# Attention with a gated expert mixture on one core: stores on another queue, transposes and sums in another order

## The chip, the cores and the metric

The kernel runs on one core of one Trainium2 chip. The metric is the time of one execution on the device, in microseconds (us). The engines are named as the profile names them: PE (TensorE; PEld is its loading of weights), DVE (VectorE), ACT (ScalarE), POOL (GpSimd) and SP (SyncE, which here only issues transfers). Each engine works through its own stream of instructions in the order in which they were written; between engines, semaphores hold an instruction until its data are there. A DMA that is issued by an engine is an instruction in that engine's stream, and what it moves goes through the queue of that engine.

## What is computed

The input `x` has 2048 tokens of 1024 features. The output is a gated mixture of two branches:

```
x  = A_x                                   # [2048, 1024]
g  = sigmoid(sum(x * gate_w))              # one number for each token
a  = softmax(q k^T / sqrt(32)) v @ wo      # 32 heads of 32, q, k, v = x @ wqkv
b  = expert lookup: 32 heads; in each, x @ w_q gives two scores over 8 keys each;
     the best pair picks a row of u and of v: sum over heads of gelu(x . u[e]) * v[e]
out = g * a + (1 - g) * b
```

All of it is float32. TensorE multiplies numbers of a shorter form (`F32R`), so each operand is split into a high part (a rounded copy) and a low part (operand minus high part), and a product is three products of parts.

## The kernel before

The program is written out by hand in one order (`tc.manual_schedule()`); what an engine does first is what comes first in the text. It has five stages.

**q and k** (trace: 6 to 378 us). The projections of q and k are computed in units: unit `u` takes one chunk of 128 output features for q and for k and half of the tokens, as a 2 x 2 block product by Strassen's scheme (Winograd's form): seven products P1 to P7 of 12 matmuls each, in the order P1, P5, P6, P2, P7, P3, P4, instead of eight. Units 0 and 8 (`KC` is 8, the units of a half) are computed plainly, as there the operands for the tokens are made; units 1 to 7 and 9 to 15 run in `unit(u)` (L473). Around the products:

- The weights of the next unit, `v = u + 1`, are prepared during unit `u`. `turns` says after which product which part is made: a name with `+` is a sum of raw blocks on VectorE (`w_sum`, L216), a name without is a split into high part (ScalarE, `w_hi`) and low part (VectorE, `w_lo`). `ready(name)` (L482) does the turn of a product. In most units a turn has a sum or a split; in units 1 and 9 the turns begin only at P2 and are denser.
- VectorE adds the products into the four output blocks `c1`, `u7`, `u4`, `u2`, from PSUM. After P2, P7, P3 and P4 one block is done, and `evac` (L248) takes it out: the high part on ScalarE, then `run_late()`, then the low part on VectorE. Put on the list `late` are the squares of the block (ScalarE, for a bound on the scores; they also end the use of the PSUM bank) and the two stores of high and low part to the DRAM tensors of q or k, 256 KB each, on ScalarE's queue. They are issued at the next `run_late()`, in the next evacuation or after P1 of the next unit. High and low parts have three buffers each (`ev`, `bufs=3`); a product takes the next of six PSUM banks.
- `fold` (L320) is another computation, put between the products to fill TensorE: the router's weights `wq` (1 MB for each of 32 steps, loaded on SP's queue into four buffers of 512 KB) times differences of keys. Two steps a call, all four quarters of a PSUM bank filled after four steps; then ScalarE copies the bank (L336), and `fold_t` (L341), called between P5 and the rest of a later unit, transposes the copy with four small matmuls on TensorE (L348), has ScalarE copy the result into the buffer named `u7` (L351), and stores it to DRAM (`WPD`) through GpSimd's queue. The block `u7` of the unit goes into the same buffer after P7 (L530). Units with an entry in `MID_FOLDS` (4, 11, 13) have a second fold, after P2.
- `hooks` puts other work at named places of certain units, for example the splitting of the second half of the tokens in unit 7.

**Router** (378 to 471 us). For 16 tiles `t` of 128 tokens, `router_mm(t)` (L702, 24 matmuls) gives the scores, and `router_step(t)` the choice of the best keys, in four steps on VectorE and GpSimd that lag behind each other. Between the tiles stand: the splitting of the tokens' third and fourth quarter (`split_rx`, at t = 1, 2, 3, 5; loads `load_rx` on SP's queue); the norms of q and k from the squares (`norms`, VectorE and a square root on ScalarE, t = 2; `spread_norms`, t = 3); `bound` (L769, t = 4), which adds up the norms with small matmuls (L771, L773), writes the bound to `cbits` and a shift for each head to DRAM; loads of the v weights on SP's queue (t = 4). At t = 8 `exact_maxima` reads `cbits` and branches.

**Values** (471 to about 631 us), **attention** (about 631 to 1657 us: for each head, scores into a ring of PSUM banks, exponentials on ScalarE, products with v, row sums), and the **output projection** (from there to the end). At the last head's end the row sums are computed on TensorE (L1335), copied by ScalarE (L1372) and stored with a DMA on SP's queue (`norm_sums`, L1369). `load_r` reads them back in another layout, `norm_r` takes reciprocals (L1383) and stores them (`RD`), and `load_rb` reads these broadcast over the partitions; the last 128 features of the attention's output are scaled with them before they can be multiplied by `wo` (L1506).

Of the kernel before, what the change touches and what calls it, by code (L numbers as in the profile page):

```python
# [18 lines left out]
H = 32  # L19
KC = D // 128  # L20
HC = KC // 2
NT = S // 128
NQ = S // 512
# [8 lines left out]
def gated_mha_peer_kernel(ctx, tc, xT, wqkv, wv, wo, wq, k12, ug, v, out):  # L32
# [8 lines left out]
    nc = tc.nc  # L41
# [14 lines left out]
    SMD = [dram.tile([4, S], F32, name=f"smd{g}") for g in range(G)]  # L56
# [17 lines left out]
    def dma(dst, src, queue=nc.sync):  # L74
        a, b = (ap.bitcast(F32) if ap.dtype == F32R else ap for ap in (dst, src))
        return queue.dma_start(a, b)  # L76
# [60 lines left out]
    def lo_of(parts, src):  # L137
        nc.vector.tensor_tensor(out=parts[1], in0=src, in1=parts[0].bitcast(F32), op=OP.subtract)  # L138
# [86 lines left out]
    def w_hi(u, name, src=None):  # L225
        hi_of(w_place(name), wraw[u][src or name])

    def w_lo(u, name, src=None):
        lo_of(AW[name], wraw[u][src or name])

    def w_parts(u, *names):
        for name in names:
            w_hi(u, name)
            w_lo(u, name)


    late = []
# [7 lines left out]
    def squares(out, src, which, c, n):  # L245
        nc.scalar.activation(out, src, AF.Square, accum_out=sq[:, which, c, n:n + 1])  # L246

    def evac(which, c, n, src, ps):  # L248
        hi, lo = (ev.tile([128, 512], F32R, name=part) for part in ("hi", "lo"))
        hi_of((hi, lo), src)  # L250
        run_late()
        lo_of((hi, lo), src)
        late.append((squares, ps, src, which, c, n))
        for dst, t in zip(QKD[which], (hi, lo)):
            late.append((dma, dst[128 * c:128 * c + 128, n * 512:(n + 1) * 512], t, nc.scalar))

    def load_kq(h, tiles):
        K, Q = tiles
# [27 lines left out]
    def product(name):  # L286
        ps = bank_at(prod_no[0] % 6)
        prod_no[0] += 1
        a, b = (m[f] for m, f in zip((AW, X), FACTORS[name]))
        for k in range(HC):  # L290
            for i, j in ((0, 0), (0, 1), (1, 0)):
                nc.tensor.matmul(ps, a[i][:, k, :], b[j][:, k, :],  # L292
                                 start=(k == 0 and i == j == 0), stop=(k == HC - 1 and i == 1))
        return ps
# [46 lines left out]
    def fold_t():  # L341
        if not pending:
            return
        gi, wt = pending.pop(0)
        b, dh = divmod(gi, 2)
        pt = bank_at(7)
        for dc in range(4):
            nc.tensor.transpose(pt[:, dc * 128:(dc + 1) * 128], wt[:, dc * 128:(dc + 1) * 128], ident)  # L348
        wt2 = ev.tile([128, 512], F32, name="u7", bufs=1)[:, :448].rearrange(
            "p (a q r) -> p a q r", a=4, q=4)  # L350
        nc.scalar.activation(wt2, pt.rearrange("p (a q r) -> p a q r", a=4, q=4)[:, :, :, :28], AF.Copy)  # L351
        dma(WPD[:, 4 * dh:4 * dh + 4, 112 * b:112 * b + 112], wt2.rearrange("p a q r -> p a (q r)"),
            nc.gpsimd)
# [119 lines left out]
    def unit(u):  # L473
        p, c, v = u // KC, CHUNK[u], u + 1
        n0 = TOK0[p] // 512
        seven = v < NUNIT and v != KC
        turns = (dict(P2=("S1+", "S3+", "A11"), P7=("S1", "S2+", "S2"), P3=("S4+", "A12"), P4=("S3", "S4"))
                 if u % KC == 1 else
                 dict(P1=("S1+", "S3+", "A11"), P5=("S1", "S2+"), P6=("S2", "S4+"), P2=("A12",),
                      P7=("S3",), P3=("S4",), P4=("A22",)))  # L480

        def ready(name):  # L482
            if not seven:
                return
            for part in turns.get(name, ()):
                if part[-1] == "+":
                    w_sum(v, part[:-1])
                else:
                    w_parts(v, part)

        def hook(name):
            for f, *a in hooks.pop((u, name), []):
                f(*a)

        def place(name):
            return ev.tile([128, 512], F32, name=name, bufs=1)

        def add(out, a, b):
            nc.vector.tensor_tensor(out=out, in0=a, in1=b, op=OP.add)  # L499

        p1 = product("P1")
        c1 = place("c1")
        nc.scalar.activation(c1, p1, AF.Copy)
        run_late()
        hook("P1")
        ready("P1")
        p5 = product("P5")
        fold_t()
        hook("P5")
        ready("P5")  # L510
        p6 = product("P6")
        u2, u4 = place("u2"), place("u4")
        hook("P6")
        add(u2, c1, p6)
        add(u4, u2, p5)
        ready("P6")
        if v + 1 < NUNIT and v + 1 != KC:
            load_w(v + 1)
        p2 = product("P2")
        hook("P2-")  # L520
        add(c1, c1, p2)
        evac(0, c, n0, c1, p2)
        if u in MID_FOLDS:
            fold()
        hook("P2")
        ready("P2")
        p7 = product("P7")
        hook("P7-")
        u7 = place("u7")
        add(u7, u4, p7)  # L530
        add(u2, u2, p7)
        evac(1, c, n0 + 1, u7, p7)
        hook("P7")
        ready("P7")
        p3 = product("P3")
        hook("P3-")
        add(u4, u4, p3)
        evac(0, c, n0 + 1, u4, p3)
        hook("P3")
        ready("P3")  # L540
        p4 = product("P4")
        add(u2, u2, p4)
        evac(1, c, n0, u2, p4)
        if u in FOLDS:
            fold(u != KC - 2)
        hook("P4")
        ready("P4")
# [143 lines left out]
    sm = Pool("sm")  # L691
# [67 lines left out]
    def norms():  # L759
        nc.vector.tensor_reduce(blk, ident.rearrange("p (j r) -> p j r", j=4), axis=AX.X, op=OP.max)  # L760
        nc.vector.tensor_reduce(amax, sq, axis=AX.X, op=OP.max)
        nc.vector.tensor_mul(pr, amax[:, 0, :], amax[:, 1, :])
        nc.scalar.activation(pr, pr, AF.Sqrt)

    def spread_norms():
        nc.vector.tensor_mul(prm, pr[:, :, None].to_broadcast([128, KC, 4]),
                             blk[:, None, :].to_broadcast([128, KC, 4]))

    def bound():  # L769
        pb = bank()  # L770
        nc.tensor.matmul(pb[:H, 0:1], prf, ones[:, 0:1], start=True, stop=True)  # L771
        pb2 = bank()
        nc.tensor.matmul(pb2[:1, :H], ones[:, 0:1], prf, start=True, stop=True)  # L773
        nc.vector.tensor_reduce(cbits, pb2[:1, :H], axis=AX.X, op=OP.max)
        cneg = bw.tile([H, 1], F32, name="cneg")
        nc.scalar.activation(cneg, pb[:H, 0:1], AF.Copy, scale=-1.0)
        for r in range(2):
            sh = bw.tile([H, 512], F32R, name=f"sh{r}", bufs=1)
            if r == 0:
                nc.vector.tensor_copy(sh, cneg.to_broadcast([H, 512]))  # L780
            else:
                nc.vector.memset(sh.bitcast(F32), 0.0)
            dma(SHD[:, r, :].rearrange("h (n s) -> h n s", n=4), sh[:, None, :].to_broadcast([H, 4, 512]))
# [63 lines left out]
    def load_rx(n, i):  # L847
        rx[n, i] = load_quarter(n, i, rz.tile([128, HC, 512], F32, name="rx", bufs=2))
# [7 lines left out]
    for t in range(NT - 1):  # L856
        router_mm(t)
        if t == 8:

            exact_maxima()  # L860
        router_step(t)
        if t == 2:
            norms()
        if t == 3:
            spread_norms()
        if t == 4:
            bound()
            load_wv(0, "xh0")
            load_wv(1, "xl0")
        if t in (1, 2, 3, 5):  # L870
            ni, ki = {1: (2, 0), 2: (2, 1), 3: (3, 0), 5: (3, 1)}[t]
            split_rx(ni, ki)
            if ni == 2:
                load_rx(3, ki)
        if t == 6:
            rz.close()
        if t >= 8 and t % 2 == 0:
            ni, ki = divmod(t // 2 - 4, 2)
            in_parts(f"B{ki + 1}{2 - ni}", x_place(f"x{'hl'[ki]}{1 + ni}"), WR[ki, 1 - ni])
# [486 lines left out]
        dma(OD[g][32 * j:32 * j + 32, :].rearrange("d (q s) -> q d s", q=NQ), o)  # L1366


    def norm_sums(h, ps):  # L1369
        g, j = divmod(h, 4)  # L1370
        o = wk.tile([128, 512], F32, name="ssb")
        ins = nc.scalar.activation(o, ps, AF.Copy)  # L1372
        dma(SMD[g][j:j + 1, :].rearrange("o (q s) -> (o q) s", q=NQ), o[::32, :])
        return ins


# [50 lines left out]
    todo = {}  # L1427
# [4 lines left out]
    for h in range(H):  # L1432
        base = h * NT
        g, j = divmod(h, 4)
# [14 lines left out]
    for k in range(2 * KC):  # L1449
        c = slice(k % 2 * D // 2, (k % 2 + 1) * D // 2)  # L1450
# [134 lines left out]
    sm = pso.tile([128, 512], F32, name="o")  # L1585
# [3 lines left out]
    for kc in range(1, KC - 1):  # L1589
        split_hi(kc + 1)  # L1590
        if kc == 1:
            norm_sums(H - 1, sm)
            load_r(G - 1)
            for n in range(2):
                load_at(n)
            pso.close()
        split_lo(kc)
        wo_mm(pa, 0, [kc], False, False)
# [155 lines left out]
```

## Time and profile before

| | |
|---|---|
| median of 3 runs | 1849.5 us (1849.14 to 1852.69) |
| profiled execution, its own time | 1848.97 us |
| its span, first to last instruction | 1847.2 us |
| mean granted TensorE clock | 0.996 |
| DMA | 345.24 MB, mean 187 GB/s |

The profiled execution is the slowest core's, here the only one's. The span is shorter than the time by 1.77 us, which lie around it. Busy times of the engines are unions of their instructions; an engine's idle time before an instruction is put down to what released it. The granted clock is the share of TensorE's clock pulses that the throttle let through in a stretch, 1.00 being full speed. Lines such as L348 are lines of the kernel above. In the chain of waits and in the timelines, times are from the start of the span.

### The profile page before, as it was taken

What the parts mean: (1) busy time and instruction counts of PE and PEld (TensorE: products, weight loads), DVE (VectorE), ACT (ScalarE), POOL (GpSimd) and SP (SyncE); (2) the same over time, 40 slices, a digit from 0 to 9 for tenths busy, and PEclk for the clock granted to TensorE, in tenths of its full rate; (3) what the DMA queues carried; (4) which work ended last, traced back from release to release, by engine and by line L of the source; (5) the groups of instructions that cost most, each with busy time, mean ns of one, the idle gap of its engine ahead of it and who ended that gap; (6) DMA issues with size and microseconds to landing.
All of it is one profiled execution on the core that took longest, in us unless ns stands there. A gap on an engine that the chain in (4) does not pass through costs nothing.

```text
span 1847.2 us, 26455 instructions
## 1 busy us (share of the span) xinstructions
PE 1823.2 (99%) x10083; PEld 1103.8 (60%) x10083; DVE 1460.9 (79%) x1258; ACT 1313.8 (71%) x1716; POOL 162.1 (9%) x230
## 2 busy tenths in 40 slices
PE   9999999999999999999999999999999999999999
PEld 6677777778888744444444444444444444447787
DVE  7765875679976888888888888888888888885575
ACT  5544554522243599999999999999999999992221
POOL 1000000024201200000000000000000000010000
PEclk9999999999999999999999999999999999999999
DMA  7787788843248777777777777778777777776872
GB/s 261 228 286 249 235 256 293 249 137 105 80 154 268 238 168 165 164 159 178 163 184 161 178 179 166 178 167 186 164 182 163 169 161 178 185 135 171 279 174 79
DMA packets 135633, 345.24 MB, mean 187 GB/s; under 512 B 17168, under 2 KB 57904, under 8 KB 116112
## 3 DMA queue, kind: packets, MB, share of 16 engines
q1 hardware_dynamic: 95696, 193.41, 35.4%
q0 software_dynamic: 17984, 112.36, 28.1%
q10 hardware_dynamic: 21824, 37.76, 6.9%
q8 instruction: 80, 1.31, 0.3%
q14 instruction: 49, 0.40, 0.1%
HBM read 171.76 MB, written 72.36 MB: 132 GB/s over the span
## 4 chain that ended last, share of the span: by engine, by line
PE 72%; DMA 5%; DVE 1%; ACT 1%; SPq 0%; issue 0%; DVEq 0%; ACTq 0%; POOLq 0%
PE ring L1301 27%; PE o L1322 25%; PE bk L947 6%; PE pa L947 6%; PE bk L709 3%; PE bk L966 2%; PE ring L1335 1%; DMA accd<-P 1%; DMA accd<-rd 1%; DMA smd<-ssb 1%; PE pa L1513 1%; DMA out<-rb 1%; DMA rx<-in_xT 1%; DMA rb<-rd 0%; SPq L76 0%; DMA V<-od 0%
## 5 line engine op out<-in xcount | busy, mean ns | idle before, releaser
L1311 ACT ACTIVATE P<-ring 128x1024 f32<-128x1024 f32 (+2 forms) x1031 | 913.1, 983 | 14.1 <-DMA accd<-P 1.5
L1351 DVE TENSOR_TENSOR acc<-acc,P 128x2048 f32<-128x2048 f32 x319 | 730.9, 2291 | 72.9 <-ACT P L1311 47.1
L1322 PE MATMUL o<-P,V 128*32 128x512 f32 x3840 | 464.8, 599 | 0.0
L1301 PE MATMUL ring<-Q,K 98*128 98x512 f32 x1024 | 272.3, 407 | 0.4 <-ACT P L1311 0.4
L1301 PE MATMUL ring<-z,z 98*128 98x512 f32 x1020 | 270.4, 407 | 0.6 <-ACT accd L1311 0.6
L1301 PEld LDWEIGHTS ring<-Q,K 98*128 98x128 f32 x1024 | 182.0, 188 | 144.9 <-ACT P L1311 73.9
L1301 PEld LDWEIGHTS ring<-z,z 98*128 98x128 f32 x1020 | 181.4, 188 | 142.4 <-ACT P L1311 72.3
L1322 PEld LDWEIGHTS o<-P,V 128*32 128x32 f32 x3840 | 98.8, 109 | 223.2 <-issue 214.5
L1344 POOL DMA_DIRECT2D accd<-P x95 | 81.5, 858 | 931.6 <-ACT P L1311 430.5
L1349 DVE TENSOR_TENSOR acc<-P,P 128x2048 f32<-128x2048 f32 x32 | 73.4, 2293 | 74.3 <-ACT P L1311 74.3
L292 PE MATMUL bk<-xh,S 128*128 128x512 f32 x336 | 83.8, 401 | 0.0
L292 PE MATMUL bk<-xh,A 128*128 128x512 f32 x336 | 82.7, 395 | 0.0
L292 PE MATMUL bk<-xl,S 128*128 128x512 f32 x336 | 80.3, 391 | 0.3 <-ACT bk L246 0.3
L292 PEld LDWEIGHTS bk<-xh,A 128*128 128x128 f32 x336 | 62.1, 188 | 23.8 <-issue 5.9
L135 ACT ACTIVATE hi<-u 128x512 fp32r<-128x512 f32 x42 | 26.5, 632 | 66.5 <-DVE u L499 64.9
L1354 DVE TENSOR_TENSOR acc<-acc,accd 128x2048 f32<-128x2048 f32 x32 | 73.1, 2285 | 0.0
L292 PEld LDWEIGHTS bk<-xh,S 128*128 128x128 f32 x336 | 64.1, 193 | 14.2 <-issue 0.8
L292 PEld LDWEIGHTS bk<-xl,S 128*128 128x128 f32 x336 | 62.8, 188 | 15.5 <-issue 1.7
L1311 ACT ACTIVATE accd<-ring 128x1024 f32<-128x1024 f32 (+2 forms) x64 | 62.2, 1032 | 1.8 <-PE ring L1301 1.7
L947 PE MATMUL pa<-woh,acc 128*128 128x512 f32 x192 | 62.2, 389 | 0.0
L138 DVE TENSOR_TENSOR A<-wraw,A 128x512 fp32r<-128x512 f32 x42 | 28.9, 688 | 33.5 <-ACT A L135 33.5
L499 DVE TENSOR_TENSOR u<-u,bk 128x512 f32<-128x512 f32 x70 | 46.6, 682 | 3.6 <-PE bk L292 2.5
(298 smaller groups left out, 2126.3 us busy)
## 6 DMA issues: line engine op xcount, KB each, us to landing
accd<-P POOLq DMA_DIRECT2D x95, 1024.0 KB, 7.6
wqt<-in_wq SPq DMA_DIRECT2D x64, 512.0 KB
wraw<-in_wqkv SPq DMA_DIRECT2D x28, 512.0 KB
kdh<-hi ACTq DMA_DIRECT2D x32, 256.0 KB
kdl<-lo ACTq DMA_DIRECT2D x32, 256.0 KB
qdh<-hi ACTq DMA_DIRECT2D x32, 256.0 KB
qdl<-lo ACTq DMA_DIRECT2D x32, 256.0 KB
z<-kdh SPq DMA_DIRECT2D x32, 256.0 KB
```

The costliest lines, as they stand in the source:

```text
L292: nc.tensor.matmul(ps, a[i][:, k, :], b[j][:, k, :], start=(k == 0 and i == j == 0), stop=(k == HC - 1 and i == 1))
L499: nc.vector.tensor_tensor(out=out, in0=a, in1=b, op=OP.add)
L709: nc.tensor.matmul(ps, x_part(a, t // 4, kc)[:, tok], b, start=first, stop=last)
L947: nc.tensor.matmul(ps, self.a[a][i][:, k, :], self.b[b][j][k], start=(not first and k == 0 and i == j == 0), stop=(k == HC - 1 and i == 1))
L966: nc.tensor.matmul(p, x_part(a, t // 4, kc)[:, tok], b, start=first, stop=last)
L1301: on_ring(nc.tensor.matmul(ring[:, i, :], K[:98, kt * 128:(kt + 1) * 128], Q[:98, qc * 512:(qc + 1) * 512], start=True, stop=True), i)
L1311: on_ring(nc.scalar.activation(P[h, kt][:, q0 * 512:(q0 + m) * 512].rearrange("p (a m) -> p a m", a=m), ring[:, i:i + m, :], AF.Exp, scale ...
L1322: nc.tensor.matmul(O[h][32 * qc:32 * qc + 32, :], Vt[g][:, kt, 32 * j:32 * j + 32], p[:, qc * 512:(qc + 1) * 512], start=(kt == 0), stop=( ...
L1344: nc.gpsimd.dma_start(ACCD[h], P[h, kt], accum_op=OP.add)
L1349: nc.vector.tensor_add(ACC[h], P[h, 0], P[h, kt])
L1351: nc.vector.tensor_add(ACC[h], ACC[h], P[h, kt])
L1354: nc.vector.tensor_add(ACC[h], ACC[h], ACCD[h])
```

## The change

Five things are moved; no arithmetic is added or left out.

1. The stores of q and k, 32 times four of 256 KB, are issued by GpSimd instead of ScalarE.
2. The evacuations after P2, P7, P3 and P4 in `unit` no longer write the low part at once. It is put on the list `held`, and `ready` writes it after the sums and high parts of its turn and before the turn's low parts. The plain evacuations of units 0 and 8 write it at once, as before.
3. In units 2 and 10 (`u % KC == 2`) `fold_t` comes after P2 instead of after P5.
4. In the router, `norms` and `spread_norms` come after the splits of their tiles, and `bound` at t = 6 instead of t = 4.
5. The last head's row sums are stored on ScalarE's queue instead of SP's.

```diff
+    held = []
+
+    def free_held():
+        for parts, src in held:
+            lo_of(parts, src)
+        held.clear()
+
-    def evac(which, c, n, src, ps):
+    def evac(which, c, n, src, ps, hold=False):
         hi, lo = (ev.tile([128, 512], F32R, name=part) for part in ("hi", "lo"))
         hi_of((hi, lo), src)
         run_late()
-        lo_of((hi, lo), src)
+        if hold:
+            held.append(((hi, lo), src))
+        else:
+            lo_of((hi, lo), src)
         late.append((squares, ps, src, which, c, n))
         for dst, t in zip(QKD[which], (hi, lo)):
-            late.append((dma, dst[128 * c:128 * c + 128, n * 512:(n + 1) * 512], t, nc.scalar))
+            late.append((dma, dst[128 * c:128 * c + 128, n * 512:(n + 1) * 512], t, nc.gpsimd))
...
         def ready(name):
-            if not seven:
-                return
-            for part in turns.get(name, ()):
+            todo = turns.get(name, ()) if seven else ()
+            for part in todo:
                 if part[-1] == "+":
                     w_sum(v, part[:-1])
                 else:
-                    w_parts(v, part)
+                    w_hi(v, part)
+            free_held()
+            for part in todo:
+                if part[-1] != "+":
+                    w_lo(v, part)
...
         p5 = product("P5")
-        fold_t()
+        if u % KC != 2:
+            fold_t()
...
         p2 = product("P2")
+        if u % KC == 2:
+            fold_t()
         hook("P2-")
         add(c1, c1, p2)
-        evac(0, c, n0, c1, p2)
+        evac(0, c, n0, c1, p2, True)
...
         router_step(t)
-        if t == 2:
-            norms()
-        if t == 3:
-            spread_norms()
+        if t == 6:
+            bound()
         if t == 4:
-            bound()
             load_wv(0, "xh0")
             load_wv(1, "xl0")
         if t in (1, 2, 3, 5):
...
             split_rx(ni, ki)
             if ni == 2:
                 load_rx(3, ki)
+        if t == 2:
+            norms()
+        if t == 3:
+            spread_norms()
...
-    def norm_sums(h, ps):
+    def norm_sums(h, ps, queue=nc.sync):
...
-        dma(SMD[g][j:j + 1, :].rearrange("o (q s) -> (o q) s", q=NQ), o[::32, :])
+        dma(SMD[g][j:j + 1, :].rearrange("o (q s) -> (o q) s", q=NQ), o[::32, :], queue)
...
-            norm_sums(H - 1, sm)
+            norm_sums(H - 1, sm, nc.scalar)
```

More of the change, by code (lines that the diff above doesn't have):

```diff
@@ L531, in unit @@
         add(u2, u2, p7)
-        evac(1, c, n0 + 1, u7, p7)
+        evac(1, c, n0 + 1, u7, p7, True)
         hook("P7")
@@ L537, in unit @@
         add(u4, u4, p3)
-        evac(0, c, n0 + 1, u4, p3)
+        evac(0, c, n0 + 1, u4, p3, True)
         hook("P3")
@@ L542, in unit @@
         add(u2, u2, p4)
-        evac(1, c, n0, u2, p4)
+        evac(1, c, n0, u2, p4, True)
         if u in FOLDS:
```

## Prediction, before the result was known

> **What bounds the kernel now.** I read the page's busy line first, then the waits of TensorE (line, whom it waited for, us in total, times, longest).
>
> ```profile
> PE 1823.2 (99%) x10083; PEld 1103.8 (60%) x10083; DVE 1460.9 (79%) x1258; ACT 1313.8 (71%) x1716; POOL 162.1 (9%) x230
> ...
> PE bk L348 <- ACT x L336: 7.9, 3, 4.0
> ...
> PE bk L771 <- DVE prm L766: 2.8, 1, 2.8
> ```
>
> TensorE is busy for 1823.2 of 1847.2 us. Its work does not change, so only its idle 24.0 us and what follows from them can be won. Two waits belong to lines that the diff moves: the fold's transposes (L348) and the bound's matmul (L771). Now the timeline of TensorE: start, length, idle time before it.
>
> ```profile
> 62.08 2.88 PE L292 MATMUL bk<-xl,S 128*128 128x512 f32 x12
> 69.00 1.11 PE L348 MATMUL bk<-ident,x 128*128 128x128 f32 x4 [4.03 <-ACT x L336]
> ...
> 74.99 2.91 PE L292 MATMUL bk<-xl,A 128*128 128x512 f32 x12
> ...
> 111.90 2.89 PE L292 MATMUL bk<-xl,S 128*128 128x512 f32 x12
> ...
> 117.83 2.88 PE L292 MATMUL bk<-xl,A 128*128 128x512 f32 x12
> ...
> 247.74 2.88 PE L292 MATMUL bk<-xh,S 128*128 128x512 f32 x12
> 253.01 0.66 PE L348 MATMUL bk<-ident,x 128*128 128x128 f32 x4 [2.39 <-ACT x L336]
> ...
> 256.26 2.88 PE L292 MATMUL bk<-xl,A 128*128 128x512 f32 x12
> ...
> 316.92 2.88 PE L292 MATMUL bk<-xh,S 128*128 128x512 f32 x12
> ...
> 324.56 2.88 PE L292 MATMUL bk<-xl,A 128*128 128x512 f32 x12
> ```
>
> Each pair runs from the start of product P5 to the start of P2, with the transposes and P6 between. Unit 4 (111.90 to 117.83) has no wait: 5.93 us. Unit 2 takes 12.91, unit 10 8.52, unit 13 7.64. So they lose 6.98, 2.59 and 1.71 us. Unit 2 loses more than its 4.03 us of idling; the windows say why (start:end, length, busy of PE, PEld, DVE, ACT, POOL, then the granted clock):
>
> ```profile
> 69.00:73.00 4.00, 4.00 (x12) 3.32 (x13) 2.66 (x5) 3.59 (x9) 0.16 (x1) 0.50 1.12 239
> 250.00:254.00 4.00, 1.61 (x10) 1.09 (x9) 2.37 (x4) 2.77 (x7) 0.00 (x0) 1.00 1.04 392
> 409.00:413.00 4.00, 4.00 (x14) 3.13 (x11) 3.93 (x6) 0.16 (x1) 1.24 (x2) 0.57 0.02 8
> ```
>
> After the wait of 4.03 us the clock was 0.50, after the bound's 2.8 us it was 0.57, after 2.39 us it stayed at 1.00. Long waits are paid twice.
>
> **Transposes behind P2 in units 2 and 10 (u % KC == 2).** Why is the copy L336 late there? ScalarE works in order, behind the evacuations of the unit before, and those wait for VectorE:
>
> ```profile
> 54.35 0.68 DVE L499 TENSOR_TENSOR c<-c,bk 128x512 f32<-128x512 f32 x1
> 55.73 0.69 DVE L138 TENSOR_TENSOR lo<-c,hi 128x512 fp32r<-128x512 f32 x1 [0.70 <-ACT hi L135]
> 56.34 1.29 DVE L223 TENSOR_TENSOR S<-wraw 128x512 f32<-128x512 f32 x2
> ...
> 66.50 0.68 DVE L499 TENSOR_TENSOR u<-u,bk 128x512 f32<-128x512 f32 x1
> ...
> 68.37 0.57 ACT L336 ACTIVATE x<-bk 128x512 f32<-128x512 f32 x1
> ...
> 69.50 0.69 DVE L138 TENSOR_TENSOR S<-S,S 128x512 fp32r<-128x512 f32 x1 [0.92 <-ACT S L135]
> ```
>
> P5 of unit 2, started at 62.08, ends some 2.7 us later, at 64.8, and the transposes then wait for 68.37 + 0.57. With P6 and P2 ahead of them they come at 64.8 + 2 x 2.72 = 70.2, after the copy even if nothing else changed. What is late in their place? The last row is the low part of S3, which P7 needs: done at 70.2, P7 due at 70.2 + 0.4 for the transposes. The low parts for P6 and P2 stand ahead of it in VectorE's order, the later one right before the add at 66.50, and P2 is due at 67.5. So each is in time, S3 barely, and the held low parts (next) bring it forward. Unit 10 is the same pattern with less lag. Gain 6.98 + 2.59 = 9.57 us, the clock penalty of unit 2 included.
>
> **Low parts held.** VectorE idles 0.70 us between an add and its low part (55.73). In units 1 and 9, where the turns have sums (56.34 is such a pair), the sums now fill that gap. That can bring the last add (66.50) and L336 about 2 us forward (three gaps of 0.70), which makes the step above safer and counts nothing by itself: an engine that is not the bound. In the other units no sum stands there: nothing. Units 7 and 15 put splits of x and of the router's weights ahead of the held part; only its store waits for that. Bounds -0.5 to +0.5, under one such gap.
>
> **Stores through GpSimd.** In unit 13 ScalarE could not get its copy out:
>
> ```profile
> 315.95 0.63 ACT L135 ACTIVATE hi<-u 128x512 fp32r<-128x512 f32 x1 [1.35 <-DVE u L499]
> ...
> 320.66 0.60 ACT L336 ACTIVATE x<-bk 128x512 f32<-128x512 f32 x1 [3.46 <-DMA wqt<-in_wq]
> ```
>
> Two store issues stand between these rows in ScalarE's stream and were held up behind weight loads. Without them L336 follows at about 317.3, before P5's end at 319.6: gain 1.71 us. What GpSimd pays is shown by the fold's own stores there:
>
> ```profile
> L76 POOL DMA_DIRECT2D wpd<-u x8: 750/757/802, 72.8 to 346.6; - x8
> ...
> DMA to landing us min/median/max: 5.1/6.7/7.8
> ```
>
> Eight stores a unit at 0.757 us are 6.1 us of GpSimd in a unit of about 20 us, on an engine 9% busy. A store now starts when its half is written, not at the next evacuation. The buffers turn over by threes: the hi of P4 needs the store of P2's, written 3 x 2.72 = 8.2 us before, landed. At 0.8 + 6.7 this just fits; at 7.8 ScalarE waits under a microsecond, which the operands' lead of a unit hides. I count 0; bounds 0 to +3.
>
> The moved transposes shorten another path: their result sits in u7's buffer, and the add into u7 after P7 must wait until GpSimd's store has landed. The store now starts two products later. VectorE lags: unit 1's P4 ended two products and a fold of 1.92 before 64.8, at 57.4, and its add ran at 66.50, nine us behind. With the held parts and the gaps it loses I reckon on five us of lag, so that the add, whose P7 ends about 73.4, is due at 78.4; the store, issued about 74.5, lands 5.1 to 7.8 us later, at 79.6 to 82.3. VectorE waits 1 to 4 us at L530. Queued behind are the adds of P7, P3, P4 and the next unit's S3. P7's bank is used again six products later (16.3 us), S3 a unit later: cover enough. If it fails, up to 3 us in each of two units.
>
> Earlier stores also meet the loads of wqt. The end fold of units 4, 11 and 13 needs 2 MB issued about 8 us before:
>
> ```profile
> 130.92 2.25 PE L331 MATMUL bk<-wqt,kpad 128*32 128x512 f32 x16
> ...
> q1 hardware_dynamic: 644, 2.31, 83.7%
> ```
>
> The first row shows such a fold 0.33 us longer than the usual 1.92; the second is the loads' queue in the window 282.0 to 290.5 (packets, MB, share of 16 engines). There is no slack: 0.5 MB of stores moved forward at 2.31 MB per 8.5 us x 83.7% of the engines (some 320 GB/s) is 1.5 us (the 0.5 MB are the two halves of P7's evacuation). Against that, the stores of the preceding unit are out of the way sooner. I take 0.2 us three times, 0.6, nearest to the 0.33 seen; bounds -1, three such 0.33, to 4.5.
>
> **Bound at t = 6, norms behind the splits.**
>
> ```profile
> 402.39 2.29 DVE L95 TENSOR_TENSOR xl<-rx,xl 128x2048 fp32r<-128x2048 f32 x1 [2.08 <-ACT xl L94]
> ...
> 408.59 0.18 DVE L766 TENSOR_TENSOR prm<-pr,blk 128x32 f32<-128x32 f32 x1
> ...
> 406.02 0.22 ACT L713 ACTIVATE xu<-bk 128x64 f32<-128x64 f32 x1 [1.75 <-PE bk L709]
> ...
> 416.42 0.22 ACT L713 ACTIVATE xu<-bk 128x64 f32<-128x64 f32 x1 [7.18 <-PE bk L709]
> ...
> 421.86 0.22 ACT L713 ACTIVATE xu<-bk 128x64 f32<-128x64 f32 x1 [3.41 <-PE bk L709]
> ```
>
> The xu copies mark the router's tiles: 5.44 us apart undisturbed (416.42 to 421.86), 10.40 across the bound. TensorE reaches the bound about 405.8 and waits for prm; two tiles later it comes at 416.7, eight us after 408.59, and prm moves by at most one split (2.29) to about 409. Moreover the 2.08 us go, in which VectorE waited for a split behind the square root. The small matmuls stay (0.23). Gain 10.40 - 5.44 - 0.23 = 4.73 us; the 1.9 beyond the idling is clock. The reader of cbits stands at t = 8, two tiles on. The loads of wv no longer queue on SP behind the shift's store.
>
> The Trainium skill, "TensorE: Matmul & The Clock Gate", "What's actually happening", puts the fall to half rate after an idle window of about 3.4 us. The row of 0.57 differs, a wait of 2.8 us sufficed; by the page the bound's wait would return 2.8 us, not 4.73, and the sum would be 1.9 smaller.
>
> **Last row sums on ScalarE's queue.** The chain, two waits of TensorE, and the loads' queue in the window 1677 to 1680:
>
> ```profile
> 1667.08 12.55 DMA smd<-ssb
> 1679.70 1.78 DMA rr<-smd
> ...
> 1688.12 1.19 PE L1506 MATMUL pa<-woh,z 128*128 128x512 f32 x4 [3.35 <-ACT z L94]
> ...
> 1725.71 3.29 PE L947 MATMUL pa<-wo_raw,z 128*128 128x512 f32 x12 [1.21 <-ACT z L94]
> ...
> q1 hardware_dynamic: 29, 0.05, 4.6%
> ```
>
> An 8 KB store takes 12.55 us behind SP's queue, of which one of the 16 engines works to the end (4.6% is under 1/16). On ScalarE's queue it passes that; but its reader rr stays on SP's queue and must pass the same engine. So only rr's own 1.78 us go: I take 1.7. The rows bound it by -0.5 (ScalarE held) and 3.35 plus a clock penalty like the bound's 1.9, 5.2; the DMA chain to 1725.71 keeps most of what exceeds 1.7.
>
> **Sum.** 9.57 + 1.71 + 4.73 + 1.7 - 0.6 = 17.1 us. The profiled execution took 1848.97 us, so 1831.9; the median of the runs shown is 0.5 higher (1849.5): I predict 1832.4.
>
> **Rivals.** (1) Something new becomes late (L530 in units 2 and 10, wqt at the folds of 4, 11 and 13): 4.5 - 0.6 + 2 x 3 = 9.9 us of the gain go again, about 1842, or less if one of them comes; speaking for it are the full loads' queue and VectorE's lag, against it the operands' lead. (2) rr slips past the busy engine: 3.5 more, about 1829. (3) The change does not take: GpSimd's landing is as late as ScalarE's blocked issue and the same waits return: 1849. (4) Slower: GpSimd's descriptor work is held up by a busy VectorE. It decides when a store holds GpSimd over 20 / 8 = 2.5 us; each 0.1 us beyond costs 8 x 0.1 x 15 units = 12 us, so 2.7 us a store gives 24 - 17 = +7, about 1856. Against it: 750 to 802 ns in eight places beside a VectorE 79% busy.
>
> The Trainium skill, "SBUF — State Buffer", "A bandwidth-pool intuition that's wrong (but worth ruling out)", has such a store go from 620 to 3100 ns beside a VectorE copy; by that, 8 x 0.6 x 15 is some 70 us lost (an estimate). The wpd row shows no trace of it.
>
> **Chances.** Forecast (1829.5 to 1835) 0.66; (1) 0.13; (2) and other larger gains 0.10; (3) 0.04; (4) and the like 0.07. Range 1826.5 to 1840: the forecast's own 1829.5 to 1835 (the bounds of the small terms, one or two at a time), most of (2) and the milder half of (1). Faster by over 0.2% (about what a measurement of this kernel can tell from no change) 0.89, within 0.04, slower 0.07.
>
> **What would show it.** Right: no idle time before L348 in any unit, granted clock 1.00 throughout 60 to 80 and near the bound, xu copies 5.4 to 5.7 us apart, GpSimd's stores at 0.75 us, rr landing at most two us sooner relative to the row sum. Wrong: TensorE waiting at L292 for bk freed by squares in unit 3, at L331 for wqt, or GpSimd's stores over 2 us.

## The result and the profile after

The changed kernel took 1841.86 us (median of 10 executions, 1837.65 to 1847.63), the kernel before 1850.8 us (10 executions, 1848.64 to 1854.85): ratio 0.9949, 95% interval 0.9934 to 0.9963. It is faster by half of what was forecast. Its executions spread over 10 us, those of before over 6; in later sets before spreads over 7.3 to 8.3 and the changed kernel over 7.5, so that difference is no finding. The profiled execution took 1842.35 us, span 1840.5. In the table below, one execution of e11, at 2241.17 us, stands far outside all others for a cause that is not known, and is left out.

The waits of TensorE on lines of the change, in the profile after (line, for whom, us in total, times, longest):

```profile
PEld bk L341 <- DMA wqt<-in_wq: 10.8, 6, 3.5
PE bk L341 <- DMA wqt<-in_wq: 5.6, 3, 2.6
```

The transposes and the bound are gone from this list. In their place stand the folds' matmuls (L341, L331 before), waiting for `wqt`. TensorE's timeline, unit 2, unit 13 and the three end folds:

```profile
60.66 2.88 PE L302 MATMUL bk<-xl,S 128*128 128x512 f32 x12
63.38 2.88 PE L302 MATMUL bk<-xh,S 128*128 128x512 f32 x12
66.10 2.89 PE L302 MATMUL bk<-xl,A 128*128 128x512 f32 x12
68.83 0.60 PE L358 MATMUL bk<-ident,x 128*128 128x128 f32 x4
...
122.50 1.95 PE L341 MATMUL bk<-wqt,kpad 128*32 128x512 f32 x12
127.04 1.05 PE L341 MATMUL bk<-wqt,kpad 128*32 128x512 f32 x4 [2.59 <-DMA wqt<-in_wq]
128.03 4.61 PE L302 MATMUL bk<-xh,A 128*128 128x512 f32 x12
...
283.84 2.10 PE L341 MATMUL bk<-wqt,kpad 128*32 128x512 f32 x12
287.92 1.24 PE L341 MATMUL bk<-wqt,kpad 128*32 128x512 f32 x4 [1.99 <-DMA wqt<-in_wq]
289.09 4.40 PE L302 MATMUL bk<-xh,A 128*128 128x512 f32 x12
...
317.70 0.60 PE L358 MATMUL bk<-ident,x 128*128 128x128 f32 x4
...
334.00 2.02 PE L341 MATMUL bk<-wqt,kpad 128*32 128x512 f32 x12
337.04 1.05 PE L341 MATMUL bk<-wqt,kpad 128*32 128x512 f32 x4 [1.01 <-DMA wqt<-in_wq]
338.02 2.37 PE L302 MATMUL bk<-xh,A 128*128 128x512 f32 x9
```

No transposes wait now. But from the end fold of unit 4 to the next product go 5.53 us (122.50 to 128.03), where an undisturbed fold takes 1.85, and that product takes 4.61 instead of 3.06, its clock having fallen: 3.68 + 1.55 = 5.23 us lost. In the same way unit 11 loses 3.40 + 1.34 and unit 13 2.17: together 12.1 us, against 0.33 before. I call this sum, over all folds of a profile, the **folds' loss** below. The windows (start:end, length, busy of PE, PEld, DVE, ACT, POOL, clock) show both sides, unit 2 at full clock and the products after the late folds:

```profile
66.00:70.00 4.00, 4.00 (x22) 3.30 (x21) 3.16 (x6) 2.96 (x7) 0.00 (x0) 1.00 0.91 346
...
128.00:132.00 4.00, 4.00 (x12) 3.13 (x11) 1.90 (x3) 1.11 (x2) 0.00 (x0) 0.57 1.01 317
289.00:293.00 4.00, 4.00 (x13) 3.17 (x12) 0.31 (x1) 0.00 (x0) 0.00 (x0) 0.62 0.99 285
412.00:416.00 4.00, 4.00 (x22) 3.02 (x21) 3.93 (x8) 0.36 (x2) 1.97 (x3) 1.00 0.66 256
```

The span is 6.7 us shorter: 1.42 in the start (unit 1 begins at 36.60 instead of 38.02), 0.28 from there to the router, 4.64 in the router's first nine tiles, -0.75 from there to the output projection, 1.11 in the projection. The 1.42 are scatter: over all profiles of this study unit 1 begins between 36.56 and 38.05, whatever the kernel. So of the 11.28 us that units 2, 10 and 13 give, the folds take all back (11.8); 0.28 is left because unit 9, whose wait of 0.28 is gone with the slower product behind it, gives another 0.6 us and small differences the rest.

### The profile page after: what moved, and what is told of

Its sections match the earlier page's. It is cut to its first block, busy times and chain, and to the rows that moved or that the text cites. A ratio compares the mean times of both kernels' runs of the same rounds, so it can differ in the third digit from the quotient of the medians.

```text
span 1840.5 us, 26554 instructions
## 1 busy us (share of the span) xinstructions
PE 1823.3 (99%) x10083; PEld 1102.1 (60%) x10083; DVE 1461.7 (79%) x1258; ACT 1312.7 (71%) x1716; POOL 231.3 (13%) x358
## 4 chain that ended last, share of the span: by engine, by line
PE 88%; DMA 6%; issue 3%; DVE 1%; ACT 1%; POOL 1%; SPq 1%; ACTq 0%; DVEq 0%; POOLq 0%
PE ring L1318 28%; PE o L1339 25%; PE bk L302 14%; PE pa L964 6%; PE bk L725 5%; PE bk L983 2%; PE bk L290 2%; DMA wqt<-in_wq 2%; PE bk L341 2%; PE ring L1352 1%; PE bk L964 1%; DMA accd<-rd 1%; PE pa L1530 1%; DMA out<-rb 1%; DMA accd<-P 1%
## 5 line engine op out<-in xcount | busy, mean ns | idle before, releaser
L964 PE MATMUL pa<-woh,acc 128*128 128x512 f32 x192 | 62.2, 389 | 0.0
L512 DVE TENSOR_TENSOR u<-u,bk 128x512 f32<-128x512 f32 x70 | 46.6, 682 | 10.0 <-PE bk L302 5.4
```

The lines of the kernel that those rows point to most:

```text
L964: nc.tensor.matmul(ps, self.a[a][i][:, k, :], self.b[b][j][k], start=(not first and k == 0 and i == j == 0), stop=(k == HC - 1 and i == 1))
```

## Experiments

Theory A: the stores, through GpSimd, are on their way while the last `wqt` load should be, and it comes late. Theory B: TensorE, which no longer stalls, is too fast for the loads, whatever queue the stores use. The results first: medians of 4 to 12 executions, with the ratio to the kernel before in the same set of runs; the last column is the folds' loss in the one profiled execution, whose own time stands beside it.

| run | median us | ratio to before (95%) | folds' loss (profiled execution) |
|---|---|---|---|
| changed kernel | 1841.86 | 0.9949 (0.9934-0.9963) | 12.1 (1842.35) |
| e1 all stores on ScalarE | 1838.19 | 0.9942 (0.9927-0.9956) | 2.5 (1836.88) |
| e2 before, stores on GpSimd | 1851.10 | 1.0006 (0.9997-1.0015) | 4.8 (1850.42) |
| e3 units 4, 11, 13 on ScalarE | 1834.12 | 0.9908 (0.9893-0.9923) | 1.5 (1836.08) |
| e4 middle fold earlier | 1833.43 | 0.9915 (0.9901-0.9928) | 2.4 (1833.31) |
| e5 GpSimd later, new tile | 1837.17 | 0.9935 (0.9922-0.9948) | 1.4 (1836.09) |
| e6 ScalarE early | 1838.41 | 0.9945 (0.9929-0.9961) | 6.0 (1834.67) |
| e7 no hold | 1837.23 | 0.9939 (0.9924-0.9953) | 4.6 (1837.95) |
| e8 e3 and e4 together | 1833.06 | 0.9916 (0.9901-0.9932) | 2.3 (1833.17) |
| e9 GpSimd later | 1830.14 | 0.9897 (0.9881-0.9912) | 0.0 (1828.36) |
| e10 changed kernel again | 1840.75 | 0.9950 (0.9935-0.9965) | 2.6 (1835.01) |
| e11 units 4, 11, 13 on SyncE | 1834.16 | 0.9914 (0.9898-0.9930) | 4.0 (1833.95) |
| e12 no hold again | 1839.57 | 0.9940 (0.9924-0.9956) | 6.6 (1838.92) |
| e13 transposes back | 1840.25 | 0.9953 (0.9936-0.9970) | 8.0 (1841.22) |
| e14 transposes alone | 1843.85 | 0.9972 (0.9960-0.9985) | 3.3 (1843.98) |
| e15 later in all units | 1841.09 | 0.9955 (0.9938-0.9972) | 4.2 (1843.30) |
| e16 e9 again | 1830.84 | 0.9910 (0.9894-0.9927) | 0.0 (1830.84) |

e10 is the changed kernel itself: the profiled execution was the fastest of its six and lost 2.6 us, the first profile, at 1842.35, lost 12.1. So the loss varies from one execution to the next by as much as the time does, and one profile is not the rule; medians decide below. The profiles agree on one thing: from unit 1 to the router the changed kernel, e3, e4, e6 to e8 and e10 to e12 all take 327.9 to 328.1 us once the folds' loss is taken off, so that in this stage nothing else differs between them.

**e1, e2: one part undone, one part alone.** `nc.gpsimd` to `nc.scalar` in `evac` of the changed kernel, and the reverse in the kernel before.

> The changed kernel with the stores of q and k back on ScalarE's queue, all else as changed. Theory A (the stores through GpSimd start earlier or take a larger share of the DMA engines, and the last wqt load of units 4, 11 and 13 comes late): the end folds' waits for wqt and the cold rows after them go from 12.2 us to under 2, the wait of 1.7 us of unit 13's fold copy returns, about 1832 us (1829 to 1836). Theory B (TensorE, about 11 us faster here, leaves the loads too little time whatever queue the stores are on): the waits stay at 8 us or more, about 1842 us.

> The kernel before with the stores of q and k through GpSimd and nothing else. Theory A: waits for wqt of about 10 to 12 us with their cold rows appear in the end folds of units 4, 11 and 13, against 1.7 us saved in unit 13: slower than before by about 10 us, 1861 us (1857 to 1864). Theory B: no such waits, 1849 us. The 9.6 us of stalls in units 2 and 10 and the 4.7 us of the router's bound stay in both.

Neither theory's number came. In e1 the folds' loss fell to 2.5 us, as A says, but the time is not clearly below the changed kernel's, because the fold's copy was held up in ScalarE's stream again, in two units instead of one (4 and 13; the expectation of e14 calls the first one 5):

```profile
109.11 0.66 PE L358 MATMUL bk<-ident,x 128*128 128x128 f32 x4 [1.82 <-ACT x L346]
...
314.41 0.66 PE L358 MATMUL bk<-ident,x 128*128 128x128 f32 x4 [1.60 <-ACT x L346]
```

In e2 the folds lost 4.8 us, not 10 to 12, and 2.3 us of waits went (unit 13's 1.51 and 0.83 of unit 10's): no difference in the time. By the times (2.3 us of waits gone, the median 1.0 longer) GpSimd's stores cost some 3 us in the kernel before, and by e9 and e10 below about 10 in the changed one, so A and B both hold a part.

**e3, e4, e8: two remedies.** Stores of `MID_FOLDS` units on `nc.scalar`; `fold()` of these units moved from behind `evac` of P2 to ahead of `load_w(v + 1)`; both.

```diff
+        store_q[0] = nc.scalar if u in MID_FOLDS else nc.gpsimd    # e3, e8
-        if u in MID_FOLDS:                                         # e4, e8
-            fold()
...
+        if u in MID_FOLDS:
+            fold()
         if v + 1 < NUNIT and v + 1 != KC:
             load_w(v + 1)
```

> The changed kernel with the stores of units 4, 11 and 13 alone on ScalarE's queue, those of the other eleven units through GpSimd. Theory A, with the competing stores those of the same unit: the waits fall below 2 us, unit 13's 1.7 us return, about 1832 us (1829 to 1836), as with all stores on ScalarE's queue. If stores of the unit before matter as much, about 5 us of the waits stay, 1836 us. Theory B: 1842 us.

> The changed kernel with the middle fold of units 4, 11 and 13 one product earlier, behind P6, and the loads that it issues ahead of the next weights' load: the last wqt load has four products instead of three ahead of its fold, and no weights' load before it in SyncE's queue. Theory A (a race of 2 MB of loads with the stores within the stretch): the waits of the end folds fall below 2 us, and 0 to 3 us come at the middle folds, whose loads have a product less: about 1832 us (1829 to 1836). If stores take whatever the engines have until they are done, at least 6 us of waits stay at one fold or the other: 1837 us or more.

> The changed kernel with both remedies: stores of units 4, 11 and 13 on ScalarE's queue and the middle fold one product earlier, ahead of the weights' load. If both only take away the same waits for wqt, 1832 us (1830 to 1835), within 2 us of either alone; each alone leaves 1.5 to 2.2 us of loss in unit 11's folds, and that is all that is left to gain. Rival: the loads, all issued earlier, crowd out the next weights' load, whose splits then wait: 1835 us or more.

All three came out as theory A has it, 16 to 16.7 us below before where the changed kernel has 8.9 and 9.6, and together no better than each alone: both take away the same loss. A 2 MB load that has one product more and goes ahead of the next weights (e4), or that has no stores of its own unit beside it at first (e3), is in time, but for 1.5 us in unit 11 of e3; in e4 the 2.4 us lie at the middle folds, whose loads have a product less. The 1.7 us of unit 13's copy, which the expectation of e3 had returning, did not return.

**e5, e9, e16, e6: start or queue?** When are the stores issued? In unit 4 of the changed kernel, middle fold at 112.22, GpSimd's issues:

```profile
113.97 0.54 POOL L76 DMA_DIRECT2D qdh<-hi  x1 [5.50 <-ACT hi L135]
114.70 0.54 POOL L76 DMA_DIRECT2D qdl<-lo  x1 [0.18 <-issue]
118.81 0.54 POOL L76 DMA_DIRECT2D kdh<-hi  x1 [3.58 <-ACT hi L135]
119.54 0.54 POOL L76 DMA_DIRECT2D kdl<-lo  x1 [0.19 <-issue]
121.98 0.54 POOL L76 DMA_DIRECT2D qdh<-hi  x1 [1.90 <-ACT hi L135]
```

and ScalarE's in the same unit before, middle fold at 120.64:

```profile
126.38 0.34 ACTq L76 DMA_DIRECT2D qdh<-hi  x1
...
129.50 0.34 ACTq L76 DMA_DIRECT2D kdh<-hi  x1
...
132.84 0.37 ACTq L76 DMA_DIRECT2D qdh<-hi  x1
```

The loads, issued about a microsecond behind the middle fold, had 4.6 us alone before and have 0.7 now, and a third pair of stores now starts ahead of the end fold, 10.3 us behind the middle one: five stores by then, where before had four. e9 keeps GpSimd's queue and takes the early start away: a one-element copy on GpSimd reads the next high part ahead of each pair's issue (and `c1` at the next unit's start).

```diff
         hi_of((hi, lo), src)
+        if store_q[0]:                      # u in MID_FOLDS
+            nc.gpsimd.tensor_copy(tick[:1, :1], hi[:1, :1].bitcast(F32))
         run_late()
```

e6 leaves the queue to ScalarE and issues there early (high part in `evac`, low part at the end of `ready`); its issues in unit 4 stand at 114.05, 114.77, 118.89, 119.62 and 122.02, with the middle fold at 112.56: 0.3 us nearer to it than in the changed kernel.

> The changed kernel, all stores through GpSimd, but in units 4, 11 and 13 each pair of stores is issued only once ScalarE has made the next pair's high part (a one-element copy on GpSimd reads it first), which is where ScalarE's stream issued them: 2 to 4 us later than in the changed kernel. Theory A1 (the early start does it): the end folds' waits go as in the run with these units' stores on ScalarE's queue, about 1834 us (1831 to 1837). Theory A2 (the queue does it, whose larger packets get more of the engines): the waits stay at 8 us or more, about 1842 us.

> The run with GpSimd's later stores, with its one-element copies into a tile that is there already: the new tile of the first version shifted what lies behind it, and the router's matmuls took 396 to 397 ns there against 389 to 391, some 3 us outside the folds. If the start time decides (that run's folds lost 1.4 us, its queue being GpSimd's as in the changed kernel): folds' loss under 2.5 us, 1834 us (1832 to 1837). If that one profile was a lucky one of a wide spread: 1838 us or more.

> The kernel with GpSimd's later stores in units 4, 11 and 13 as it was, on this call's chip: 1830 us (1828 to 1833), folds' loss under 1.5 us, if the first result was typical; 1834 us, as with these units' stores on ScalarE's queue, if it was a lucky one.

> The changed kernel with the stores of units 4, 11 and 13 on ScalarE's queue but early: the high part's right behind its conversion, the low part's at the end of the same step, so at about the times at which GpSimd issued them. Theory A1 (early start): the waits for wqt come back on this queue, 6 us or more in the three end folds, 1840 us or more. Theory A2 (the queue): no more than 2 us of them, about 1834 us (1831 to 1837).

The start decides between these. With GpSimd's queue and the later start the folds lose nothing in two profiles, and the time is 1830.14 and 1830.84 us, the first 10.6 below the changed kernel in the same set of runs: the fastest version of all. The three end folds of e9:

```profile
122.61 1.92 PE L343 MATMUL bk<-wqt,kpad 128*32 128x512 f32 x16
...
278.71 1.92 PE L343 MATMUL bk<-wqt,kpad 128*32 128x512 f32 x16
...
324.14 1.92 PE L343 MATMUL bk<-wqt,kpad 128*32 128x512 f32 x16
```

e5, the same start with a new tile for the copies, loses 1.4 us at the folds but takes 1837.17; the last section takes that up. With ScalarE's queue and the early start (e6) the time is 1838.41, by its ratio not to be told from the changed kernel, and clearly above e3 (0.9945 against 0.9908), which differs by the start alone. Between ScalarE's queue and GpSimd's no difference is shown. In e9's unit 4 the first pair goes 5.3 us later against the middle fold (112.33):

```profile
119.34 0.55 POOL L76 DMA_DIRECT2D qdh<-hi  x1
119.88 0.54 POOL L76 DMA_DIRECT2D qdl<-lo  x1
...
122.51 0.54 POOL L76 DMA_DIRECT2D kdh<-hi  x1
```

What the queues move shows in unit 11, from the middle fold's end to the end fold (queue, packets, MB, share of 16 engines; q1 holds the loads, q0 GpSimd's stores). The changed kernel, 275.4 to 283.9, and then the stretch 283.9 to 289 in which the fold waits:

```profile
q1 hardware_dynamic: 574, 2.10, 77.2%
q0 software_dynamic: 160, 0.53, 20.8%
...
q0 software_dynamic: 267, 0.89, 93.2%
q1 hardware_dynamic: 81, 0.26, 14.2%
```

and e9, 270.2 to 278.7:

```profile
q1 hardware_dynamic: 642, 2.31, 85.3%
q0 software_dynamic: 96, 0.35, 10.0%
```

The loads' 2.31 MB by the end fold, what they had before, had become 2.10, and the missing piece then crept: while TensorE waited for it, the engines gave stores 93.2% of their time and the load 14.2% (a packet counts whole where it starts, so the two exceed 100%). The creeping is not in every execution. In e10, the same kernel with the same issue times, the loads had only 2.00 MB by the end fold of unit 11 (271.8 to 280.2), and yet it lost just 0.4 us:

```profile
280.19 2.33 PE L341 MATMUL bk<-wqt,kpad 128*32 128x512 f32 x16
```

So the early start opens the race, and what decides within it how fast the last piece comes is not known.

**e11: stores behind the loads.** `store_q[0] = nc.sync if u in MID_FOLDS else nc.gpsimd`.

> The changed kernel with the stores of units 4, 11 and 13 on SyncE's queue, behind the wqt loads that it has issued before them, and as early as GpSimd issued them. If a store hurts by standing in another queue than the loads, so that the engines serve both by turns, the folds' loss goes under 2 us although the stores are issued early: 1834 us (1832 to 1837). If any early store costs the loads their share: 6 us or more of loss, 1840 us. Rival on the other side: SyncE, waiting for a low part, issues the next loads late, and the loss moves to the next unit's folds.

The time is that of the first case, the profile's 4.0 us of loss lie between the two. An early store in the loads' own queue costs 6.6 us less than through GpSimd (e10, on the same chip). Part of that can be the start: behind the loads in SyncE's stream the first pair goes 3.2 to 4.1 us after the middle fold, in the changed kernel after 1.75; the later stores go about as early as there. The Trainium skill, "DMA: Bandwidth & Descriptors", "Queues, rings and completion order", says that an engine takes turns between the queue rows that have work, a packet at a time: by that, stores on any second queue take turns with the load (e6, and the 93.2% above), and those behind it in its own queue do not. The times of e6 and e11 fit that; turns as such are not shown, as the rows do not say what each engine had left to move.

**e15: later in all units.** As e9, with `store_q[0] = True` in every unit.

> The kernel with GpSimd's later stores in units 4, 11 and 13, the fastest so far, with the stores held back in the same way in all units. If an early start of a store is worth nothing anywhere: the same 1830 us (1828 to 1832). Rival: elsewhere the buffers of the high parts come free later, ScalarE waits, and the operands of a unit come late: 1834 us or more.

The rival came, 10 us above e16. ScalarE's timeline in unit 3:

```profile
109.08 0.63 ACT L135 ACTIVATE hi<-u 128x512 fp32r<-128x512 f32 x1 [4.31 <-DMA qdh<-hi]
...
110.23 0.58 ACT L348 ACTIVATE x<-bk 128x512 f32<-128x512 f32 x1
```

The fourth high part of the unit waits 4.31 us for the first one's store, held back, to leave its buffer; behind it stands the fold's copy, and unit 4's transposes then wait 3.97 us for that. With the slower clock behind that wait this is some 6.4 us of the profile; another 4.1 come at the end fold of unit 11, although its stores are late too. So in a unit like 3 the early start is needed.

**e7, e10, e12: the hold.** `evac(..., True)` to `evac(...)` in `unit`; e10 without edit.

> The changed kernel without the hold: each low part directly behind its high part, as before the change. The prediction priced the hold at 0 (within 0.5 us); by that and theory A1 the waits of about 12 us stay and the time is 1842 us (1838 to 1845). Rival: the hold is what makes the waits longer here than in the kernel before with GpSimd's stores alone (about 5 us of loss there); then they fall to about 5 us and the time to 1835 us.

> The changed kernel as it is, on this call's chip, to compare with the others of the call and to see a second profile of it: 1842 us (1839 to 1845), end folds' loss 8 to 12 us, if the first profile was typical of it. Rival: the first profile, at 1842.35 us in a spread of 10 us, showed more than the usual loss; then about 5 us of it here and 1838 us.

> The changed kernel without the hold once more, beside the changed kernel itself on the same chip. Its instructions differ from the changed kernel's in order only in units 1, 7 and 9, where the held parts stand behind sums or other parts, so theory A1 says no difference: both about 1842, or both about 1838 us. Rival: the hold costs 4 us or more, this one 1837 us and the changed kernel 1842 us.

Beside each other on one chip the two kernels take 1839.57 and 1840.75 us: no difference that this measurement shows. e7's first 1837.23 was no sign of one.

**e13, e14: the transposes.** `fold_t()` back behind P5 in all units of the changed kernel; the move alone in the kernel before.

> The changed kernel with the transposes of units 2 and 10 back behind P5, all else as changed: their stalls return, 9.6 us by the prediction's working, less what the hold takes off them. Open question: GpSimd's early stores cost some 3.5 us in the kernel before and about 10 in the changed one. Theory A3 (the stalls gave the loads time, their return takes wqt waits away): about 5 us of folds' loss, 1845 us (1843 to 1847). Rival (the loss is the same with and without stalls, the difference lies elsewhere): folds' loss near 10 us, 1850 us.

> The kernel before with the transposes of units 2 and 10 behind P2 and nothing else, the stores on ScalarE's queue. By the prediction's working 9.6 us faster than before: 1840.5 us. Theory A3: TensorE, ahead by that much, meets waits for wqt or a fold copy held up in ScalarE's stream (units 5 and 13 had 3.4 us of these with all other parts of the change in place), so only 4 to 7 us come, 1843 to 1846 us.

In e13 the stalls did not return, so the expectation's premise failed: unit 10 has none, unit 2 one of 1.59 us.

```profile
66.20 0.65 PE L358 MATMUL bk<-ident,x 128*128 128x128 f32 x4 [1.59 <-ACT x L346]
```

GpSimd's stores alone (e2) left 3.94 us and 1.56 us of idling there; the hold, the only other part of the change in this stage, took the rest. So the hold and the move do the same work: the move alone takes both stalls (e14), the hold all but 1.59 us. e14 is 5.5 us faster than before: 9.57 by the prediction's working, less 2.9 lost at the folds and 1.5 to a late fold copy in unit 4. With ScalarE's late stores a faster TensorE pays too: theory B's part. How the changed kernel's 10 us divide between early start and missing stalls is not settled further, since e13 kept the stalls away.

## Why the prediction was wrong, step by step

**The step that failed** is the meeting of the stores with the loads of `wqt`: "I take 0.2 us three times, 0.6, nearest to the 0.33 seen; bounds -1, three such 0.33, to 4.5." It cost 12.1 - 0.33 = 11.8 us in the profiled execution, which at 1842.35 us lies near the median, and about 10 by the medians of e9 and e10. The place, the units and the mechanism were named; the size was wrong, for two reasons. The working priced 0.5 MB moved forward at the mean rate of the transfers. But the rows of unit 4 show both pairs that were there before moved forward, by 4.0 and 2.3 us, and a fifth store added ahead of the end fold, 1.3 MB in all, so that of the 4.6 us that the loads had alone 0.7 are left. That the length of this sharing decides, and not the bytes moved, is argued from e9 and e6; a price per us of it these runs do not give, as e10's 2.6 us with the same start show. And the bound of 4.5 us has no clock in it, although the same text had measured that long waits are paid twice: 2.9 of the 12.1 us are cold clock. That the first rival's 1842 us came is luck in part: 6 of its 9.9 us were to be L530's wait, which cost nothing. With the folds' loss gone the rest of the sum holds: e9 and e16 are 20.2 and 18.5 us below before, where 17.7 were said without this term. By their profiles 16.4 us of that lie in units 1 to 15 and the first nine router tiles, 16.0 said for the two; the remainder is mostly scatter of the start and the projection.

The other steps:

- **Transposes, 9.57:** the stalls went, at full clock. That the hold "counts nothing by itself" was wrong in attribution: with the transposes left in place it removes most of the same stall (e13 against e2), as it brings unit 2's copy of the bank 2.5 us forward, from 68.11 to 65.57; about 2 were said. In the sum nothing changes.
- **Unit 13, 1.71:** went. With TensorE faster, this part is worth more: e1 has 1.82 + 1.60.
- **GpSimd's issues:** 0.54 us, not the 0.757 taken, and no delay beside VectorE; the slower rival has nothing for it.

```profile
L76 POOL DMA_DIRECT2D qdh<-hi x32: 539/540/542, 41.9 to 377.4; - x32
```

- **L530's wait** (L512 after) was worked out as 1 to 4 us in each of two units. It came in unit 10 alone, 3.5 us, and cost TensorE nothing; in unit 2 there is none. The other 0.45 us of the row stand in a later unit, where before had 0.41:

```profile
DVE u L512 <- DMA wpd<-u: 4.0, 2, 3.5
```

- **The buffers that turn over by threes** were counted at 0, up to +3. Right for the change; e15 shows the price when the cover is gone.
- **Bound, 4.73:** the first nine tiles take 49.89 us instead of 54.53: 4.64. The xu copies across the bound are 5.43 and 5.92 apart:

```profile
409.61 0.22 ACT L729 ACTIVATE xu<-bk 128x64 f32<-128x64 f32 x1 [5.22 <-PE bk L725]
415.04 0.22 ACT L729 ACTIVATE xu<-bk 128x64 f32<-128x64 f32 x1 [3.41 <-PE bk L725]
420.96 0.22 ACT L729 ACTIVATE xu<-bk 128x64 f32<-128x64 f32 x1 [5.55 <-PE bk L725]
```

- **Row sums, 1.7:** 1.11 in the profile. Its path was read wrong. Not the reader's 1.78 us went, it takes 2.31; the store lands in 8.54 us instead of 12.55, and the reader ends 10.9 us after the store's issue instead of 14.4, 3.5 sooner, where at most two were said; in kind this is the second rival. The wait of 3.35 us at L1506 is gone. But the last wait (L964, L947 before) grows from 1.21 to 3.24, and the product behind it takes 4.54 us instead of 3.29: as the prediction said, the chain of transfers up to there keeps what exceeds its 1.7.

```profile
1661.49 8.54 DMA smd<-ssb
1670.10 2.31 DMA rr<-smd
```

Over the 15 profiles with this part the time from the first output product to the end is 185.8 us on average (183.2 to 190.0), over the three without 186.8: about 1 us, within the scatter.

## What to carry to other kernels

A transfer that frees an issuing engine also changes when the bytes move: before stores are started earlier, find every load that a later step waits for in the same stretch, and count how long it would have the DMA engines alone, then and now. Starting a store early pays where its buffer is wanted again and hurts where a load is due, so the right start can differ from unit to unit. Where the executions of one kernel spread, one profile shows one draw; compare medians, and read the profile for the place.

## What the runs showed of the hardware

- e5 and e9 differ only in whether the one-element copies write a new 4-byte tile, which may shift what is placed behind it, or one that was there. e5 took 1837.17 us, e9 1830.14. The same matmuls of the router from its tenth tile on, in e5 and in the changed kernel (count, busy us, mean ns):

```profile
L731 PE MATMUL bk<-wph,xl 128*128 128x512 f32 x57 | 19.1, 396 | 0.0
```

```profile
L725 PE MATMUL bk<-wph,xl 128*128 128x512 f32 x57 | 18.8, 389 | 0.0
```

  But e9's first nine router tiles took 50.02 us against e5's 51.39, so the copies are not what slows it. That the placement does was not tried by itself. Between the two profiles the router makes 2.4 of 7.7 us and the folds 1.4; most of the rest is the scatter of the projection, 2.6.
- The clock fell after folds that came 3.40 and 3.68 us late, and not after 3.35 (e6, unit 11) or 3.36 (e12, unit 11). The Trainium skill, "TensorE: Matmul & The Clock Gate", "What's actually happening", has the clock fall after an idle window of about 3.4 us. How late a fold is, is no idle window, though: it is spread over waits with matmuls between them. The longest stretch without a matmul was 1.99 and 2.59 us where the clock fell (units 11 and 4 of the changed kernel), and 1.85 and 2.23 us where it stayed, all shorter than that window, so these rows do not agree with it:

```profile
284.46 1.05 PE L347 MATMUL bk<-wqt,kpad 128*32 128x512 f32 x4 [1.85 <-DMA wqt<-in_wq]
```

```profile
285.17 1.05 PE L341 MATMUL bk<-wqt,kpad 128*32 128x512 f32 x4 [2.23 <-DMA wqt<-in_wq]
```

  So neither the lateness nor the longest stretch gives a rule here: 1.99 us sufficed once and 2.23 did not, and of two folds later than all of these, the one 4.08 us late (e15, unit 11) left the clock at 1.00, while the one 4.71 late (e13, unit 11) cost 0.82 more.
